# Attention and a leaky-ReLU MLP on one core: more blocks by seven products, keys transposed in place, and a written order for five stages

## The chip, the cores and the metric

The kernel runs on one core of one Trainium2 chip. The metric is the device time of one execution in microseconds (us); a run's time is compared with runs of the other kernel on the same chip. Five engines matter here: TensorE (PE in the profile, its weight loads PEld), VectorE (DVE), ScalarE (ACT), GpSimd (POOL, which issues the loads from DRAM) and SyncE (SP, which issues the DMA transposes and the stores). All transfers share 16 DMA engines.

## The reference

```python
def _attn_ref(q, k, v, is_retrieval, n_sink, window):      # q, k, v: 4 x 8 x 768 x 64
    scores = scale * np.matmul(q, k.transpose(0, 1, 3, 2))
    ...
    causal = rel >= 0
    stream_keep = causal & (is_sink | in_win)              # 4 sinks, window of 64
    mask = np.where(retr[0, :, 0, 0, None, None], full_mask, stream_mask)
    scores = np.where(mask[None, :, :, :], scores, -1000000000.0)
    ...
    return np.matmul(a, v)                                 # a: softmax of the scores

def _moe_ref(x, w_in, w_out):                              # 3072 x 512, 512 x 2048, 2048 x 512
    h = x @ w_in
    g = np.maximum(0.01 * h, h)
    return (g @ w_out)
```

Heads 0, 2 and 6 see all earlier positions; the five others see four sinks and a window of 64. The attention's output, heads side by side, is x of the MLP.

## The kernel before, in words

**Tiling.** The 3072 rows are cut into eight chunks of 384 queries, numbered 0 to 7 in the order of the list `ORDER`: chunks 0 and 2 are the two halves of batch 0, 1 and 3 of batch 1, 4 and 5 of batch 2, 6 and 7 of batch 3. Everything is bf16 with fp32 accumulation in eight PSUM banks, two under each of four tags (`ph`, `psS`, `po`, `py`).

**Stages.** From stage n = 2 on (the loop at the end of the kernel), stage n holds on TensorE, interleaved: the attention of chunk n + 1 (class `Attention`; its slots are "a" below), the first matmul of the MLP of chunk n (`in_slots`), and the second matmul of earlier chunks (`Pair`, whose half units are the list `outs`). The instructions of an engine run in the order in which the Python code writes them (the schedule is manual), and each DMA queue issues in that order too. The lists are mixed by `merge`, which spreads by estimated costs, and the last microseconds of a stage are set apart (`last_of`, `tail`, `keep`), with most attention slots ahead of them.

**The first matmul** comes in two forms. A tick (line 597) is 4 matmuls of 384 columns for 128 of the 2048 hidden units, emptied by one activation (line 600). A block of 512 hidden units can instead be made by seven products (class `Quad`, line 686): 7 units of 4 matmuls of 192 columns, with sums of weights (`in_sum`) and of activations (`x_sum`, four subtractions in `x_sums`, line 652), three ScalarE copies (700), three VectorE additions (714) and four activations (693). `BY_SEVEN` says which blocks are made so: two each of chunks 4, 6 and 7. A tick or a quad reads all of `xts[n]`, the transposed output of the attention of chunk n, four pieces of 384 columns, one for each pair of heads.

**How a chunk's x gets there.** When a pair of heads is through, `finish` takes a reciprocal and a product on VectorE (lines 423, 425), and `x_t` issues a DMA transpose from SP's queue (line 430). This is so from chunk 3 on (`cross=True`); earlier chunks are transposed on TensorE.

**Keys and queries.** `load_qk` (line 116) loads a chunk's keys and queries with GpSimd's queue, three DMAs each, into the single buffers `kb` and `qb`. `turn_dma` (line 248) transposes them from SP's queue into `kd` and `qd`. A matmul contracts over 128 partitions, two heads, so the keys of a head stand in a tile whose other 64 partitions are zero: `kt[i][0]` and `kt[i][1]` for even and odd heads of batches of parity i. `spreads` (line 264) copies the transposed keys from `kd` there by six VectorE copies per chunk, and for a new batch two small copies fill the sink keys `ksink` (lines 290 and 294). In stage n the order on SP's queue is: `turn_dma(n + 2)`, keys ahead of queries, then the x transposes of the attention of chunk n + 1, with the output stores (line 834) among them.

**GpSimd's queue** waits in order too: `load_qk(n + 3)` waits until the transposes of the chunk before have read the buffers, `load_v` (line 123) can be held back by a one-element copy (`hold`, lines 121 and 1173).

## Time and profile before

| | |
|---|---|
| time, median of 3 runs | 222.63 us (222.37 to 224.13) |
| profiled execution: span from first to last instruction | 219.4 us; the median run is 3.2 us longer (the profiled execution's own time outside the span is not given) |
| busy: PE / PEld / DVE / ACT / POOL | 212.3 / 168.7 / 144.5 / 147.0 / 72.6 us |
| DMA packets | 112732, 28.90 MB |
| stages 2, 3, 4 on TensorE | from 69.0, 89.6 and 109.3 us |
| stages 5, 6, 7 on TensorE, and the tail of `outs` | from 138.9, 159.3, 188.7 and 203.7 us |

How to read it: "L597 PE" is line 597 on TensorE. A matmul's own duration in the profile overlaps the next one's, so the pace of TensorE is read from the starts of successive rows (the chain of waits prints those), not from the mean duration. "DMA kd<-kb" is a transfer by the names of its tiles. The digits of a line in 40 slices are tenths of busy time in slices of 5.5 us.

### The profile page before, as it was taken

To read this page: it belongs to the slowest core of one execution; us is meant where nothing else is said; L and a number is where in the kernel's file an instruction comes from. 1 tells how busy PE (TensorE), PEld (TensorE's weight loads), DVE (VectorE), ACT (ScalarE), POOL (GpSimd) and SP (SyncE) were. 2 spreads that over 40 slices of the span, in tenths; PEclk is the share of its full clock that TensorE was granted. 3 is DMA by queue.
4 is the path that set the end of the run, shared out by engine and by line. 5 is a ranking of instruction groups with operands and counts; after the bars stand their busy time and mean duration, and the time that the engine had idled before them with its cause. 6 is when DMAs were issued, how large, how long until landed. Compare 5 with 4: busy or idle time off the path is not lost.

```text
span 219.4 us, 6062 instructions
## 1 busy us (share of the span) xinstructions
PE 212.3 (97%) x2432; PEld 168.7 (77%) x2432; DVE 144.5 (66%) x392; ACT 147.0 (67%) x335; POOL 72.6 (33%) x91
## 2 busy tenths in 40 slices
PE   7799999999999999999999999999999999999993
PEld 5579775688888777876688888777787888878893
DVE  6685886949699696757267875664473846626653
ACT  4766956743876996477679786687478886567220
POOL 8998542059406906309056402700000000000000
PEclk9999999999999999999999999999999999999999
DMA  9999999999999999999999996993320131200222
GB/s 131 150 174 180 178 207 190 174 170 143 174 98 255 178 141 150 155 227 125 152 170 158 136 143 176 156 183 51 81 96 16 55 87 21 96 0 3 96 107 89
DMA packets 112732, 28.90 MB, mean 132 GB/s; under 512 B 102208, under 2 KB 109760, under 8 KB 112704
## 3 DMA queue, kind: packets, MB, share of 16 engines
q0 software_dynamic: 78080, 13.37, 85.0%
q1 hardware_dynamic: 33280, 14.65, 35.4%
q10 hardware_dynamic: 1344, 0.50, 1.2%
q8 instruction: 19, 0.31, 0.6%
q14 instruction: 9, 0.07, 0.1%
HBM read 27.30 MB, written 6.29 MB: 153 GB/s over the span
## 4 chain that ended last, share of the span: by engine, by line
PE 88%; DMA 6%; POOL 2%; DVE 1%; issue 1%; POOLq 0%
PE ph L597 26%; PE py L800 20%; PE po L326 8%; PE py L779 8%; DMA va<-in_v_dram 6%; PE psS L357 5%; PE ph L686 4%; PE psS L392 3%; PE psS L597 2%; PE po L779 2%; PE po L800 2%; PE ph L779 1%; POOL va L123 1%; PE psS L686 1%; PE po L686 1%; PE psS L779 1%
## 5 line engine op out<-in xcount | busy, mean ns | idle before, releaser
L597 PE MATMUL ph<-xt,w_in_bf 128*128 128x384 bf16 x352 | 68.9, 326 | 0.0
L600 ACT ACTIVATE g_all<-ph 128x384 bf16<-128x384 f32 x88 | 43.4, 493 | 21.1 <-PE ph L597 18.5
L597 PEld LDWEIGHTS <-w_in_bf 128*128 128x128 bf16 x384 | 34.0, 97 | 17.4 <-issue 0.9
L362 ACT ACTIVATE at<-psS 128x384 bf16<-128x384 f32 x76 | 36.0, 490 | 9.0 <-PE psS L357 5.7
L800 PEld LDWEIGHTS <-sum 128*128 128x128 bf16 x256 | 23.8, 98 | 4.1
L116 POOL DMA_DIRECT2D kb<-in_k_dram x21 | 18.6, 908 | 20.9 <-DMA kd<-kb 20.4
L357 PE MATMUL psS<-qd,kt 128*128 128x384 bf16 (+2 forms) x90 | 23.0, 294 | 0.0
L123 POOL DMA_DIRECT2D va<-in_v_dram x24 | 21.4, 914 | 0.9 <-DVE xs L573 0.7
L116 POOL DMA_DIRECT2D qb<-in_q_dram x21 | 18.7, 920 | 3.9 <-DMA w_in_bf<-in_moe_w_in_dram 1.7
L326 PE MATMUL po<-va,at 128*128 128x65 bf16 x228 | 19.6, 194 | 0.3 <-DMA va<-in_v_dram 0.3
L800 PEld LDWEIGHTS <-g_all 128*128 128x128 bf16 x192 | 18.0, 98 | 2.3
L401 DVE TENSOR_TENSOR ats<-ats,m_win 128x384 bf16<-128x384 bf16 x35 | 13.1, 375 | 10.0 <-ACT ats L397 9.8
L800 PE MATMUL py<-w_sum,sum 128*128 128x256 bf16 x120 | 17.7, 272 | 0.0
L326 PEld LDWEIGHTS <-at 128*128 128x128 bf16 x234 | 14.4, 98 | 3.8 <-issue 0.5
L397 ACT ACTIVATE ats<-psS 128x384 bf16<-128x384 f32 x33 | 16.0, 494 | 1.8 <-PE psS L392 1.5
L761 DVE TENSOR_TENSOR sum<-g_all 128x1024 bf16<-128x1024 bf16 x24 | 16.4, 684 | 0.0
L800 PE MATMUL py<-w_out_bf,g_all 128*128 128x256 bf16 x112 | 16.1, 272 | 0.0
L800 PE MATMUL py<-w_out_bf,sum 128*128 128x256 bf16 x120 | 15.7, 273 | 0.0
L425 DVE TENSOR_TENSOR xs<-po,linv 128x384 bf16<-128x384 f32 x27 | 15.1, 558 | 0.9
L779 PEld LDWEIGHTS <-sum 128*128 128x128 bf16 x152 | 13.1, 98 | 1.6 <-issue 0.2
L264 DVE COPY kt<-kd 64x512 bf16<-64x512 bf16 x36 | 12.7, 362 | 1.3 <-DMA kd<-kb 0.9
L326 PEld LDWEIGHTS <-ats 128*128 128x128 bf16 x210 | 10.3, 97 | 2.5 <-DVE ats L401 0.2
(244 smaller groups left out, 402.0 us busy)
## 6 DMA issues: line engine op xcount, KB each, us to landing
out_dram<-o SPq DMA_DIRECT2D x23, 256.0 KB, 3.7
va<-in_v_dram POOLq DMA_DIRECT2D x24, 128.0 KB, 6.9
kb<-in_k_dram POOLq DMA_DIRECT2D x21, 128.0 KB, 6.5
qb<-in_q_dram POOLq DMA_DIRECT2D x21, 128.0 KB, 6.7
w_out_bf<-in_moe_w_out_dram POOLq DMA_DIRECT2D x4, 512.0 KB, 12.4
vb<-va SPq DMA_DIRECT2D x8, 170.6 KB, 3.6
w_in_bf<-in_moe_w_in_dram POOLq DMA_DIRECT2D x2, 512.0 KB, 8.3
w_in_bf<-in_moe_w_in_dram POOLq DMA_DIRECT2D x4, 256.0 KB, 7.9
```

What stands on the lines that cost most here:

```text
L116: nc.gpsimd.dma_start(out=t[:, g], in_=nat[nm][b, c, :, :, g])
L123: nc.gpsimd.dma_start(out=va[b][:, 3 * c + g, :, 0:D], in_=nat["v"][b, c, :, :, g])
L326: nc.tensor.matmul(o, lhsT=lhsT, rhs=rhs, start=first, stop=False, skip_group_check=True)
L357: nc.tensor.matmul(s[:, off : off + w], lhsT=kt[i][hh][:, p, 128 * kj : 128 * kj + 128], rhs=q_of(n, p, lo, CH), start=(j == 0), stop=(j = ...
L362: nc.scalar.activation(out=a[:, 0:off], in_=s[:, 0:off], func=ACTF.Exp, scale=SM)
L397: nc.scalar.activation(out=av_, in_=s[:, 0:CH].rearrange("p (j e f) -> p j e f", j=3, e=2), func=ACTF.Exp, scale=SM)
L425: nc.vector.tensor_tensor(xs[:], po[:, :, :, 0:D], linv.to_broadcast([128, 3, 2, D]), op=ALU.mult)
L597: nc.tensor.matmul(ph[:, 0:CH], lhsT=w_in_bf[:, g, 128 * t : 128 * t + 128], rhs=xts[n][:, g, :] if n else xts[0][:, :, g, :], start=(g == ...
L600: nc.scalar.activation(out=g_all[:, slab(n) : slab(n) + 3, t, :], in_=ph[:, 0:CH].rearrange("p (j t) -> p j t", j=3), func=ACTF.Prelu, alp ...
L761: nc.vector.tensor_tensor(self.s[i], x, y, op=op)
L779: nc.tensor.matmul(s[:, 0 : c1 - c0], lhsT=lhs[:, j, :], rhs=rhs[:, j, c0:c1], start=first and j == 0, stop=(j == NH - 1), skip_group_chec ...
L800: nc.tensor.matmul(s, lhsT=lhs[:, j, :], rhs=rhs[:, j, :], start=u in ("P1", "P2", "P5") and j == 0, stop=(j == NH - 1), skip_group_check= ...
```

## The change

1. `BY_SEVEN` gets two blocks each of chunks 3 and 5: four quads replace sixteen ticks. Each of the two chunks needs its `x_sums`.
2. The keys of chunks 4 to 7 are loaded by six DMAs, even and odd heads apart, into one tile `kz` whose other halves are zeroed once (two memsets on VectorE after the copies of chunk 3's keys). Three DMA transposes, each of eight 128 x 128 blocks where there were four, write straight into `kts`. The VectorE copies of `spreads` are gone for these chunks; the two copies of sink keys stay. `kz` takes the memory of the two `kd` buffers. The keys of chunk 4 are loaded after the memsets, at the end of the part ahead of the loop, and not with its queries; the keys of chunks 5 to 7 wait for the transposes of the chunk before to have read `kz`.
3. Stages 3 to 7 are no longer mixed by `merge`: `WOVEN` writes out their order, one letter for an item: a an attention slot, p a half unit of `outs`, t a tick, A and B the units of the two quads, x the four subtractions of `x_sums`, e a copy of sink keys, v the shift of V (in stage 4, the transposes of chunk 7's keys).
4. In woven stages a quad runs its products in another order, puts P2, P5 and P3 into one bank under the tag `po`, and adds P5 straight from that bank.

```diff
--- before.py
+++ after.py
@@ -79,7 +79,10 @@
     m_win0 = bf("m_win0", 6, 64)
     m_sink = one.tile([128, H], FP32, name="m_sink")
     hold = bf("hold", 1)
-    kt = [[bf(f"kt{i}_{hh}", 4, S) for hh in range(2)] for i in range(2)]
+    kts = [bf(f"kt{i}", 4, 2, S) for i in range(2)]
+    kt = [[t[:, :, hh, :] for hh in range(2)] for t in kts]
+    kz = bf("kz", 3, 4, 2, 128)
+    halves = [kz.rearrange("p g q h t -> p (g q h t)")[:, 1536 * i : 1536 * i + 1536] for i in range(2)]
     va = [bf(f"va{i}", 6, H, D + 1) for i in range(2)] * 2
     vb = [bf(f"vb{i}", 5, H - 1, D + 1) for i in range(2)] * 2
     vs = [bf(f"vs{i}", H, D + 1) for i in range(2)]
@@ -95,7 +98,7 @@
 
     raw = {}
 
-    k0 = rot.tile([128, 3, H, D], BF16, name="k0", tag="kd", bufs=2)
+    k0 = halves[0].rearrange("p (g h d) -> p g h d", g=3, h=H)
     q0 = rot.tile([128, 3, H, D], BF16, name="q0", tag="qd", bufs=3)
     f0 = {nm: rot.tile([128, DM], FP32, name="o", tag="o", bufs=4).rearrange("p (h d) -> p h d", h=H) for nm in ("k", "q")}
 
@@ -110,6 +113,12 @@
     def load_qk(n, nms="kq"):
         b, c = ORDER[n]
         for nm in nms:
+            if nm == "k" and n > 3:
+                for g in range(3):
+                    w = kz[:, g].rearrange("p q h t -> p (q h t)").rearrange("p (q x) -> p q x", q=4)
+                    for hh in range(2):
+                        nc.gpsimd.dma_start(out=w[:, :, 192 * hh : 192 * hh + D], in_=nat[nm][b, c, :, hh:H:2, g])
+                continue
             t = rot.tile([128, 3, H, D], BF16, name=f"{nm}b", tag=f"{nm}b", bufs=1)
             raw[nm, n] = t
             for g in range(3):
@@ -237,8 +246,16 @@
             move(eng, kt[0][h][:, :, 128 * j : 128 * j + 128], pt[:], h)
 
     def turn_dma(n, nms="kq"):
+        b, c = ORDER[n]
         for nm in nms:
-            dst = rot.tile([128, 3, 4, 128], BF16, name=f"{nm}d", tag=f"{nm}d", bufs=3 if nm == "q" else 2)
+            if nm == "k" and n > 3:
+                for g in range(3):
+                    o = CH * c + 128 * g
+                    nc.sync.dma_start_transpose(out=kts[b % 2].rearrange("p q h t -> p (q h) t")[:, :, o : o + 128],
+                                                in_=kz[:, g].rearrange("p q h t -> p (q h t)"))
+                continue
+            dst = rot.tile([128, 3, 4, 128], BF16, name="qd", tag="qd", bufs=3) if nm == "q" else \
+                halves[n % 2].rearrange("p (g q t) -> p g q t", g=3, q=4)
             if nm == "q":
                 qx[n] = dst
             else:
@@ -263,7 +280,7 @@
             o = CH * c + 128 * g
             nc.vector.tensor_copy(kt[b % 2][hh][r, :, o : o + 128], raw["kx", n][r, g])
 
-        order = [(g, hh) for hh in range(2) for g in range(3)] if n == 3 else [(g, hh) for g in range(3) for hh in range(2)]
+        order = [] if n > 3 else [(g, hh) for hh in range(2) for g in range(3)] if n == 3 else [(g, hh) for g in range(3) for hh in range(2)]
         r = [lambda g=g, hh=hh: spread(g, hh) for g, hh in order]
         if c == 0:
             r += sink_keys_by(b)
@@ -484,8 +501,9 @@
                 self.at = rot.tile([128, H, 128], BF16, name="at8", tag="sum", bufs=6)
             else:
                 self.blocks = [(kj, h) for kj in range(j, -1, -1) for h in RETR] + [None]
-                tag, bufs = ("sum", 6) if j == 1 else ("kd", 2)
-                self.at = rot.tile([128, len(self.blocks), 128], BF16, name="at_first", tag=tag, bufs=bufs)
+                n = len(self.blocks)
+                self.at = rot.tile([128, n, 128], BF16, name="at_first", tag="sum", bufs=6) if j == 1 else \
+                    halves[1][:, 0 : 128 * n].rearrange("p (n t) -> p n t", n=n)
 
         def key(self, h, k0):
             return kt[0][h % 2][:, h // 2, k0 : k0 + 128]
@@ -581,7 +599,14 @@
 
 
     done = [0] * NCH
-    BY_SEVEN = {4: (0, 1), 6: (0, 1), 7: (0, 1)}
+    BY_SEVEN = {3: (0, 1), 4: (0, 1), 5: (0, 1), 6: (0, 1), 7: (0, 1)}
+    WOVEN = {
+        3: "xaptpAAapaAtAaAapaAAAapBtaapptBaBtpBBataBBtBpppvaaapppt",
+        4: "pxaAapppAatpaAatAApaepAaApaatpaaAtpaaBBapaBtpaBapBppaeppaBpBpatapatppavptpppBpp",
+        5: "xaaAAptpaAatAAapaApAttaaBApBaBptBaapptpvaaBpptpaBBpBtp",
+        6: "xppaaAptAaappAaAtAapaApaatpaaBtAaapBApaaptppaaBppBBapatBpBaaptppBppaappppptp",
+        7: "txAtppAptpApBAttBApBpBAABtpBptpBtpBpApp",
+    }
 
     def slab(n):
         return 4 if n % 2 else n // 2 % 2
@@ -602,6 +627,8 @@
 
         ks = BY_SEVEN.get(n, ())
         ticks = [costing(0.65, lambda t=t: tick(t)) for t in range(NG) if t // 4 not in ks]
+        if n in WOVEN:
+            return {"t": ticks, **{"ABCD"[j]: Quad(n, k, ("psS" if j < 2 else "ph") if n + 1 == NCH else "ph", True).slots() for j, k in enumerate(ks)}}
         if n + 1 == NCH:
             several = [Quad(n, k, tag).slots() for k, tag in zip(ks, ("psS", "po", "ph"))]
             if len(ks) > 2:
@@ -651,24 +678,31 @@
         for i, y, z in ((1, b(0, 1), b(0, 0)), (2, b(1, 1), t[:, 0]), (3, b(1, 1), b(0, 1)), (4, b(1, 0), t[:, 1])):
             nc.vector.tensor_tensor(t[:, i - 1], y, z, op=ALU.subtract)
         x_sum[n] = t
-        if n + 1 == NCH:
-            temps[n] = [rot.tile([128, 2, CH], FP32, name=nm, tag=tag, bufs=bufs) for nm, tag, bufs in
-                        (("p1s", "kd", 2), ("us", "kd", 2), ("u3s", "kb", 1))]
+        if n in (6, 7) and len(BY_SEVEN[n]) > 0:
+            three = [t.bitcast(FP32).rearrange("p (x t) -> p x t", x=2) for t in
+                     (*halves, rot.tile([128, 1536], BF16, name="u3s", tag="kb", bufs=1)[:])]
+            temps[n] = [[t[:, x] for t in three] for x in range(2)]
+
 
     class Quad:
 
 
-        def __init__(self, n, k, tag):
-            self.n, self.k, self.tag = n, k, tag
+        ORDERS = (("P1", "P6", "P7", "P4", "P2", "P5", "P3"), ("P1", "P2", "P6", "P5", "P7", "P4", "P3"))
+
+        def __init__(self, n, k, tag, woven=False):
+            self.n, self.k, self.tag, self.woven = n, k, tag, woven
             self.bank, self.late = {}, []
 
         def slots(self):
-            return [costing(0.33, lambda u=u: self.unit(u)) for u in ("P1", "P6", "P7", "P4", "P2", "P5", "P3")] + [costing(0.0, lambda: self.late.pop()())]
+            return [costing(0.33, lambda u=u: self.unit(u)) for u in self.ORDERS[self.woven]] + [costing(0.0, lambda: self.settle())]
+
+        def settle(self):
+            while self.late:
+                self.late.pop()()
 
         def unit(self, u):
             n, k = self.n, self.k
-            while self.late:
-                self.late.pop()()
+            self.settle()
             t = x_sum[n]
             x = xts[n].rearrange("p g (j e t) -> p g j e t", j=3, e=2)
             b = lambda a, e: x[:, KH * a : KH * a + KH, :, e, :]
@@ -678,8 +712,10 @@
                             "P7": (q(3), t[:, 2], "y"), "P5": (q(1), t[:, 0], "x"), "P4": (w(1, 1), t[:, 3], "y"),
                             "P3": (q(4), b(1, 1), "x")}[u]
             first = u in ("P1", "P2", "P5")
-            if first:
-                self.bank[at] = bank(self.tag, [128, 512], FP32)
+            if u == "P5" and self.woven:
+                self.bank[at] = self.bank["a"]
+            elif first:
+                self.bank[at] = bank("po" if u == "P2" and self.woven else self.tag, [128, 512], FP32)
             s = self.bank[at]
             for m in range(2):
                 for g in range(KH):
@@ -696,23 +732,25 @@
             if not self.left:
                 done[self.n] += 4
 
+        def add(self, u, s):
+            t, m, e = {"P2": (self.p1, 0, 0), "P5": (self.u3, 1, 1), "P3": (self.u, 0, 1)}[u]
+            nc.vector.tensor_tensor(t, s, t, op=ALU.add)
+            self.late.append(lambda: self.out(t, m, e))
+
         def empty(self, u, s):
-            copy = lambda o: nc.scalar.activation(out=o, in_=s, func=ACTF.Copy)
             if u == "P1":
                 self.left = 4
-                self.p1, self.u, self.u3 = (t[:, self.k] for t in temps[n]) if n in temps and self.k < 2 else \
-                    (rot.tile([128, CH], FP32, name=nm, tag=nm, bufs=1)[:] for nm in ("p1q", "uq", "u3q"))
-                copy(self.p1)
-            elif u == "P6":
-                copy(self.u)
-            elif u == "P7":
-                copy(self.u3)
-            elif u == "P4":
+                own = temps.get(self.n, ())
+                self.p1, self.u, self.u3 = own[self.k % 3] if self.k % 3 < len(own) else \
+                    [rot.tile([128, CH], FP32, name=nm, tag=nm, bufs=1)[:] for nm in ("p1q", "uq", "u3q")]
+            if u in ("P1", "P6", "P7"):
+                nc.scalar.activation(out={"P1": self.p1, "P6": self.u, "P7": self.u3}[u], in_=s, func=ACTF.Copy)
+            if u == "P4":
                 self.out(s, 1, 0)
-            else:
-                t, m, e = {"P2": (self.p1, 0, 0), "P5": (self.u3, 1, 1), "P3": (self.u, 0, 1)}[u]
-                nc.vector.tensor_tensor(t, s, t, op=ALU.add)
-                self.late.append(lambda: self.out(t, m, e))
+            elif u == "P7" and self.woven:
+                self.add("P5", self.bank["x"][:, 0:CH])
+            elif u in ("P2", "P3") or u == "P5" and not self.woven:
+                self.add(u, s)
 
     def in_tile(t0, j, tag="ph", nt=4):
         ph = bank(tag, [128, 4, 128], FP32)
@@ -1093,7 +1131,7 @@
     run(p1[:14], steps(0, ("P1",)), p1[14:])
     fourth = weight_sums(1)
     turn_dma(3)
-    load_qk(4)
+    load_qk(4, "q")
     run(steps(1, ("P1",)))
     run(steps(0, ("P2", "P6")))
     fourth()
@@ -1115,6 +1153,9 @@
     turn_thirds(3, (1, 2), "psS", "a")
     sp, keep = spreads(3), tail(m2[at:], a2[-7:])
     run(keep[:-5], sp[:3], keep[-5:], sp[3:])
+    for hh in range(2):
+        nc.vector.memset(kz[:, :, :, hh, 64 - 64 * hh : 128 - 64 * hh], 0.0)
+    load_qk(4, "k")
     load_v(4)
 
     for n in range(2, NCH):
@@ -1125,7 +1166,7 @@
                 sink_values(ORDER[n + 2][0], nc.gpsimd)
             turn_dma(n + 2, "q" if n == 5 else "kq")
             if n == 3:
-                load_v(n + 2, behind=raw["kx", n + 2][0:1, 0, 0, 0:1])
+                load_v(n + 2, behind=kt[ORDER[n + 2][0] % 2][0][0:1, 0, CH * ORDER[n + 2][1] : CH * ORDER[n + 2][1] + 1])
             if n == 4:
                 v_shift(n + 2)
             extra = spreads(n + 2)
@@ -1133,10 +1174,27 @@
                 load_qk(n + 3, "k" if n > 2 else "kq")
         if n + 1 < NCH:
             a = Attention(n + 1, cross=True).slots(lag=2 if n > 3 else 3)
-            a = into(a, extra) if n > 2 else a
+            a = into(a, extra) if n > 2 and n not in WOVEN else a
         if n == 2:
             a = [(lambda f=f, i=(6, 9, 12, 15).index(j): (f(), in_sums(0, i + 1))) if j in (6, 9, 12, 15) else f for j, f in enumerate(a)]
         ins = in_slots(n)
+        if n in WOVEN:
+            lists = {"a": a, "p": outs, "x": [lambda: x_sums(n)], "e": [], "v": [lambda: v_shift(n + 2)], **ins}
+            if n > 2:
+                lists["e"] += extra
+            if n == 4:
+                lists["v"] = [lambda: turn_dma(7, "k")]
+            if n == 5 and len(BY_SEVEN.get(7, ())) > 2:
+                lists["e"] += [lambda i=i: in_sums(1, i + 1) for i in range(4)]
+            for c in WOVEN[n]:
+                lists[c].pop(0)()
+            assert not any(lists[c] for c in "aptABCDe" if c in lists)
+            if n in (3, 4):
+                nc.gpsimd.tensor_copy(hold[0:1, :], xts[n + 1][0:1, 3, 0:1])
+                load_qk(n + 3, "q")
+                load_v(n + 3)
+            outs = [f for k in range(3 * n // 2, 3 * n // 2 + 1 + n % 2) for f in steps(k)]
+            continue
         if n == 7:
             x_sums(n)
         if n == 3:
@@ -1156,7 +1214,7 @@
             at = last_of(ms, 3.5)
             ms, keep = ms[:at], tail(ms[at:-2], a[-3:]) + ms[-2:]
             keep.insert(2, lambda: v_shift(4, nc.scalar))
-            a = a[:-7] + [f for i in range(4) for f in (a[i - 7], *extra[2 * i : 2 * i + 2])]
+            a = a[:-7] + [f for i in range(4) for f in (a[i - 7], *extra[i : i + 1])]
         elif a:
             at = last_of(ms, 3.2 if n == 3 else 5.8)
             ms, keep = ms[:at], ms[at:]
```

## The prediction

> **What bounds the kernel now.** I read the page first, then TensorE's waits, then the chain of waits, then busy time by stage.
>
> ```profile
> span 219.4 us, 6062 instructions
> PE 212.3 (97%) x2432; PEld 168.7 (77%) x2432; DVE 144.5 (66%) x392; ACT 147.0 (67%) x335; POOL 72.6 (33%) x91
> DMA  9999999999999999999999996993320131200222
> ```
>
> ```profile
> PE psS L156 <- DVE first L939: 1.1, 1, 1.1
> ```
>
> This is TensorE's longest wait, in the opening; the same view from 30 us on has no row at all. A busy TensorE could still be a slow one, so the pace must be seen in the chain:
>
> ```profile
> 132.29 0.65 PE ph L597 x4
> 132.94 0.33 PE ph L686 x4
> 133.27 0.44 PE py L800 x4
> ```
>
> Each row starts where the one before ends. TensorE streams without gaps here. So a gain can come only from columns that are not streamed, and any wait put on TensorE adds in full. The stages concerned:
>
> ```profile
> core 0: us, PE busy (x) PEld busy (x) DVE busy (x) ACT busy (x) POOL busy (x), PEclk, DMA share, GB/s
> 89.60:109.30 19.70, 19.70 (x214) 14.35 (x213) 11.11 (x32) 14.14 (x31) 5.51 (x7) 1.00 1.64 167
> 109.30:138.90 29.60, 29.60 (x351) 24.85 (x349) 20.71 (x53) 21.57 (x51) 12.14 (x16) 1.00 1.56 153
> 138.90:159.30 20.40, 20.40 (x220) 15.12 (x219) 10.81 (x33) 14.10 (x32) 2.41 (x3) 1.00 0.96 117
> ```
>
> These are stages 3, 4 and 5: TensorE is full in all three, at full clock, and stage 4, which has two quads already, is as full as stage 3, which has none. A better written order has nothing to win there. The other number to keep is the DMA share, over 1 until stage 5: transfers queue behind one another.
>
> **The change part by part.** *Four quads for sixteen ticks.* A tick is 0.65 us (first row of the chain above), four of them 2.60. A unit of a quad is 0.33, seven 2.31. Each quad saves 0.29, four save **1.2 us**. What empties their banks:
>
> ```profile
> L600 ACT ACTIVATE g_all<-ph 128x384 bf16<-128x384 f32 x88 | 43.4, 493 | 21.1 <-PE ph L597 18.5 <-PE po L326 1.1 <-DVE at L367 0.3
> L700 ACT ACTIVATE uq<-ph 128x384 f32<-128x384 f32 x4 | 2.0, 495 | 0.4 <-PE ph L686 0.4
> L714 DVE TENSOR_TENSOR uq<-ph,uq 128x384 f32<-128x384 f32 x4 | 2.2, 552 | 1.2 <-PE ph L686 1.2
> L652 DVE TENSOR_TENSOR x_sum<-xt 128x384 bf16<-128x384 bf16 x6 | 2.1, 350 | 0.0
> L264 DVE COPY kt<-kd 64x512 bf16<-64x512 bf16 x36 | 12.7, 362 | 1.3 <-DMA kd<-kb 0.9
> ```
>
> On ScalarE a quad costs three copies and four activations of nearly the same shape, 7 x 0.5 = 3.5 us, for four activations of 0.49: 1.5 more, 3.1 more in stages 3 and 5. ScalarE goes from 14.1 of 19.7 us (72%) to about 17.2 of 19.1 (90%). VectorE gets 6 x 0.55 and 4 x 0.35 per chunk, 4.7 us, and loses 6 x 0.36, 2.2: 2.5 more, about 71%. I cost both at nothing, because TensorE is the cover and both stay below it; P5 starts in the bank of P2 and so waits for the addition (0.55); the written order puts P6 and another item, 0.66 us or more, between them. If bursts break that cover, the nearest row is one activation late, 0.5 us, a few times: 0 to 1.5 us, of which I take 0.
>
> *The copies of keys go.* VectorE was not the bound, so the 24 copies (8.7 us) are worth nothing by themselves.
>
> *The keys of chunk 4 start later.* The memsets stand behind the last copies of chunk 3's keys, and the load stands behind the memsets.
>
> ```profile
> 70.10 1.52 DVE L264 COPY kt<-kd 64x512 bf16<-64x512 bf16 x3
> ```
>
> ```profile
> 68.00 2.63 POOL L116 DMA_DIRECT2D kb<-in_k_dram  x3 [10.61 <-DMA kd<-kb]
> 70.59 2.66 POOL L116 DMA_DIRECT2D qb<-in_q_dram  x3
> 73.19 2.70 POOL L123 DMA_DIRECT2D va<-in_v_dram  x3
> 84.22 2.70 POOL L116 DMA_DIRECT2D kb<-in_k_dram  x3 [7.38 <-DMA kd<-kb]
> ```
>
> ```profile
> L183 DVE MEMSET kt<- 64x768 uint32 x4 | 2.8, 698 | 0.8 <-issue 0.8
> L140 POOL DMA_DIRECT2D w_in_bf<-in_moe_w_in_dram x6 | 4.6, 776 | 0.3 <-issue 0.2
> ```
>
> The copies end at 71.6. A memset of kt is 768 words in 0.70 us, one of kz 384 words, so two take 0.8: 72.4. Queries now go first, at 68.0. Six half-sized key DMAs follow; each issue lies between 0.45 (half of 0.9) and 0.9, and w_in's 0.78 is the nearest: 72.4 to 77.0. The values of chunk 4 come behind, 4 us later than before. A key load was in flight 5.9 us:
>
> ```profile
> kb<-in_k_dram POOLq DMA_DIRECT2D x3, 128.0 KB, 5.9
> ```
>
> Two DMAs make a third. The second of the first third is issued at 73.2 and lands at 79.1, that of the last at 76.2 and 82.1.
>
> ```profile
> 73.79 3.96 SPq L248 DMA_TRANSPOSE kd<-kb  x3
> 78.28 4.11 SPq L248 DMA_TRANSPOSE qd<-qb  x1
> 82.50 6.84 SPq L430 DMA_TRANSPOSE xt<-xs  x4
> ```
>
> SP's queue, which issued the first row at 73.8, now waits until 79.1. Behind the waiting transposes stand the queries' transposes and all four x transposes of chunk 3. The issue took about 1.3 us each, the queries' one 4.1 while the queue was full. So the keys end at 83.4, the queries at 84.7 to 87.5, and three x transposes at 88.6 to 91.4. The fourth was ready at 88.0 before (the product below plus its 0.56): SP holds it up by 0.6 to 3.4 us, or by nothing if the loads land a little sooner. I take 0, since SP has no other work then.
>
> How long eight blocks fly no row shows. Alone, three blocks took 2.3 us and twelve 3.7 (rows below); I take 3.2 alone, and the crowded 7.3 as the upper end. For chunks 5 to 7 the longer issue on GpSimd (4.6 us for 2.7) and on SP hides in idle time: the table of stages has GpSimd busy for 12.1 of 29.6 us in stage 4 and 2.4 of 20.4 in stage 5.
>
> *A tick stands fourth in stage 3.* Before, ten half units of `outs` stood ahead of the first tick of chunk 3; now the order is x, a, p, t.
>
> ```profile
> 85.23 0.25 PE L326 MATMUL po<-va,at 128*128 128x65 bf16 x3
> 86.90 0.26 PE L326 MATMUL po<-vs,at_sink 128*128 128x65 bf16 x3
> 89.61 0.33 PE L357 MATMUL psS<-qd,kt 128*128 128x384 bf16 x1
> 96.01 0.81 PE L597 MATMUL ph<-xt,w_in_bf 128*128 128x384 bf16 x4
> ```
>
> ```profile
> 87.42 0.56 DVE L425 TENSOR_TENSOR xs<-po,linv 128x384 bf16<-128x384 f32 x1
> ```
>
> Attention of chunk 3 ends at 87.0, its last product at 88.0, and its transpose was issued at once. Stage 3 starts at 89.61; a score (0.16) and a half unit (0.44) later, at **90.2**, TensorE stands at the tick, which needs that transpose. It had time until 96.0 before. How long does it fly? Two answers, for 88.0 to 88.1 and for 133 to 134:
>
> ```profile
> q0 software_dynamic: 117, 0.01, 76.0%
> xt<-xs SPq DMA_TRANSPOSE x1, 6.6
> ```
>
> ```profile
> xt<-xs SPq DMA_TRANSPOSE x1, 2.3
> ```
>
> and, for the four of chunk 3 together:
>
> ```profile
> DMA to landing us min/median/max: 3.8/5.2/6.6
> ```
>
> Beside loads it took 6.6 us, alone 2.3. With 6.6 it lands at 94.6, and TensorE waits **4.4 us**; with 2.3, at 90.3, 0.1; with 6.6 and SP 3.4 late, at 98.0, 7.8. I take 6.6, the row of this very transfer: loads of chunk 5 are again in flight, and twelve more key blocks stand ahead of it. VectorE waits with it, since x is first in its queue, but the masks behind x belong to slots that TensorE reaches later.
>
> The Trainium skill ("DMA: Bandwidth & Descriptors", queues, rings and completion order) says that each DMA engine takes turns, packet by packet, between the queues that have work. By that alone a transpose beside one loading queue should need about twice its lone time, 4.6 us, an estimate; the wait would be 2.4 and the total 223.8 us. The 6.6 of this trace is longer, since its own queue was not empty either.
>
> *Later boundaries.* At 3 to 4, three half units and a tick (2.0) and then about 2.6 us stand between the last slot and the first unit that needs the last transpose; product and flight take 1.0 + 2.3 to 6.6: 0 to 3.0. I take 0, because the code holds GpSimd's next loads until this very transpose has landed, so it should fly nearly alone. Into 5 to 7 the distance is 3.3 to 4.8 against the lone 3.3: 0.
>
> **Sum** on the profiled execution: 219.4 - 1.2 + 4.4 = 222.6 us of span, 3.2 up. The median run stands 3.2 us above the span, so **225.8 us**.
>
> **The rivals.** *A. The last x transpose flies almost alone.* Keys of chunk 5 may be loaded only after the transposes of chunk 4's keys have read `kz`, so GpSimd could start them later than 84.2, and its own load queue could be nearly empty at 88. For it: the lone 2.3 at 133, and the 3.8 of an earlier one of these four. Against it: first transposes that land by 84 release those loads just then. It decides when the flight is under 3.4 us (a wait under 1.2); then the wait is 0.1 to 1.2, and the time 221.5 to 222.6: not slower, slightly faster. I put 222.0.
>
> *B. The sink-key copy blocks VectorE.* The two copies now wait for the transposes themselves, in VectorE's order ahead of the last masks of stage 2.
>
> ```profile
> 81.47 0.58 DVE L264 COPY kt<-kd 64x512 bf16<-64x512 bf16 x2
> 82.31 0.23 DVE L367 TENSOR_TENSOR at<-at,m_caus 128x128 bf16<-128x128 bf16 x1 [0.27 <-ACT at L362]
> ```
>
> ```profile
> kd<-kb SPq DMA_TRANSPOSE x3, 7.3
> kd<-kb SPq DMA_TRANSPOSE x1, 3.7
> ```
>
> VectorE would stand at the copy at 81.5. The first third, issued at 79.1, lands at 82.3 by the lone 3.2 or at 86.4 by the crowded 7.3. The values that need the mask were multiplied at 85.2 (row above), and copy and mask take 0.6, so it decides from a landing at 84.6 on. At the crowded end TensorE loses 1.8 us, and one mask more behind the second copy, 2.5 in all, ahead of stage 3; the x transpose is as much later, with the same wait behind it: 225.8 + 2.5 = 228.3 us.
>
> *C. ScalarE becomes the bound* in stages 3 and 5, 90% busy with two banks for each use: 1.5 us on top of a short wait at the tick, 224 to 227.
>
> **How the numbers follow.** A measurement of this kernel tells about 1% from no change, 2.2 us: 220.4 to 224.9. Forecast 0.45, with waits of 2.5 to 6 us, of which 0.10 fall below 224.9; A 0.32, all within 1%, save 0.02 beyond it; B 0.15, slower; C 0.08, half of it slower. Faster 0.02, within 1% 0.44, slower 0.54. Range: from A's lower end, 221.3, to a little above B, 229.0. The forecast's own range is 223.9 to 227.4.
>
> **What would show it.** Right: a TensorE gap of 3 to 6 us at the first line 597 of stage 3, ended by the DMA xt; stage 4 to 7 without gaps; quad units at 0.33 us; SP waiting for the key load until about 79. Wrong: no gap there (A), a VectorE wait at line 290 for the key transposes with a TensorE gap before stage 3 (B), gaps spread over stages 3 and 5 that end with ScalarE (C), or a span shorter than 218 us, which no term of mine allows.

## The result, and the profile after

The kernel after took **230.73 us** (median of 6 runs, 228.94 to 232.5) beside 223.38 us (222.11 to 228.0) for the kernel before in the same comparison: ratio 1.033, with a 95% interval of 1.0269 to 1.0392. It is slower by 7.35 us. (Times here and below are medians over all runs of a kernel, while the ratios leave out runs of more than 1.5% above its fastest, so the two can differ by a few tenths of a per cent.) The forecast was 225.8, with a range that ended at 229.0. The sign was right, the size was too small.

The profiled execution took 231.75 us, of which 229.5 are span, 10.1 more than before. From its page: the span, the busy times, and the line of the clock in 40 slices.

```profile
span 229.5 us, 6197 instructions
PE 216.1 (94%) x2480; PEld 173.8 (76%) x2480; DVE 146.4 (64%) x390; ACT 149.4 (65%) x347; POOL 80.3 (35%) x103
...
PEclk9999999999999999859999999999999999999999
```

The line of the clock has a notch: slices 17 and 18 show 8 and 5 where all others show 9. TensorE was busy longer than before, though it streams fewer columns. This is the first sign that something other than a wait was added. TensorE's waits from 30 us on, a view that had no row at all before:

```profile
PE ph L622 <- DMA xt<-xs: 6.5, 5, 2.1
```

Line 622 is the tick (597 before). Where those waits lie, TensorE's timeline shows (start, length, instruction, idle time before it in brackets):

```profile
90.76 0.60 PE L838 MATMUL py<-w_out_bf,g_all 128*128 128x256 bf16 x4
93.45 0.34 PE L622 MATMUL ph<-xt,w_in_bf 128*128 128x384 bf16 x1 [2.09 <-DMA xt<-xs]
95.10 0.32 PE L622 MATMUL ph<-xt,w_in_bf 128*128 128x384 bf16 x1 [1.32 <-DMA xt<-xs]
96.17 0.48 PE L622 MATMUL ph<-xt,w_in_bf 128*128 128x384 bf16 x1 [0.74 <-DMA xt<-xs]
97.51 0.48 PE L622 MATMUL ph<-xt,w_in_bf 128*128 128x384 bf16 x1 [0.86 <-DMA xt<-xs]
97.78 1.06 PE L838 MATMUL py<-w_out_bf,g_all 128*128 128x256 bf16 x4
98.64 0.84 PE L722 MATMUL ph<-xt,w_in_bf 128*128 128x192 bf16 x4
99.28 0.84 PE L722 MATMUL po<-xt,w_in_bf 128*128 128x192 bf16 x4
...
171.41 0.32 PE L622 MATMUL ph<-xt,w_in_bf 128*128 128x384 bf16 x1 [1.51 <-DMA xt<-xs]
```

The first tick of stage 3 stands fourth, as written, and each of its four matmuls waits for its own piece of x. The half unit of `outs` ahead of it is done at 91.2 (90.76 and 0.44); the next unit starts at 97.78, where 91.85 was due. Then see what follows: the two units of a quad stand 0.64 us apart (98.64 to 99.28), not 0.33. TensorE is running at half speed. Busy time by stretch, with the granted clock in the column ahead of the last two:

```profile
95.70:102.50 6.80, 5.47 (x32) 4.00 (x32) 2.81 (x8) 2.71 (x7) 1.00 (x2) 0.50 1.54 238
102.90:116.00 13.10, 13.10 (x171) 11.00 (x169) 7.76 (x21) 11.42 (x29) 5.86 (x8) 1.00 1.26 108
116.00:146.00 30.00, 30.00 (x362) 24.86 (x360) 19.36 (x48) 21.99 (x53) 11.20 (x14) 1.00 1.62 151
146.00:169.20 23.20, 23.20 (x276) 19.58 (x274) 15.18 (x40) 17.27 (x43) 5.49 (x7) 1.00 1.34 163
```

For 6.8 us the clock was 0.50. After that the rest of stage 3 and stages 4 and 5 are as full as before: the quads themselves cost TensorE no waits here, although ScalarE is busy for 11.42 of 13.10 us (87%).

I took the start of every matmul against the pace of its form (0.162 us for 384 columns, 0.109 for 256, 0.082 for 192, and so on), so that columns, gaps and slow clock come apart:

| span of the profiled execution | us |
|---|---|
| before | 219.4 |
| columns streamed: 112 matmuls of 192 columns for 64 of 384 | -1.2 |
| gaps at the first tick of stage 3, 0.2 to 5.8 | +5.6 |
| matmuls at half clock | +2.4 |
| gap at the tick of stage 6 | +1.7 |
| first 30 us | +0.7 |
| rest, each piece under 0.4, and rounding | +0.9 |
| after | 229.5 |

These are the sizes of one execution. In a second profile of the kernel after (part 9) the gaps at the tick of stage 3 came to 3.5 us and the half clock to 1.6, and other waits stood in their place.

### The profile page after: what moved, and what is told of

It reads as the page before. It is cut to its first block, busy times and chain, and to the rows that moved or that the text cites. A ratio compares the mean times of both kernels' runs of the same rounds, so it can differ in the third digit from the quotient of the medians.

```text
span 229.5 us, 6197 instructions
## 1 busy us (share of the span) xinstructions
PE 216.1 (94%) x2480; PEld 173.8 (76%) x2480; DVE 146.4 (64%) x390; ACT 149.4 (65%) x347; POOL 80.3 (35%) x103
## 4 chain that ended last, share of the span: by engine, by line
PE 82%; DMA 11%; DVE 3%; POOL 2%; issue 1%; ACT 0%; POOLq 0%
PE ph L622 19%; PE py L838 19%; PE po L343 7%; PE py L817 7%; DMA va<-in_v_dram 6%; PE psS L374 5%; DMA xt<-xs 5%; PE ph L722 5%; PE po L722 4%; PE psS L622 2%; PE psS L409 2%; PE po L817 2%; PE po L838 2%; PE ph L817 1%; PE psS L722 1%; POOL va L132 1%
## 5 line engine op out<-in xcount | busy, mean ns | idle before, releaser
L622 PE MATMUL ph<-xt,w_in_bf 128*128 128x384 bf16 x288 | 59.1, 328 | 6.5 <-DMA xt<-xs 6.5
L625 ACT ACTIVATE g_all<-ph 128x384 bf16<-128x384 f32 x72 | 35.5, 493 | 28.9 <-PE ph L622 27.2
L622 PEld LDWEIGHTS <-w_in_bf 128*128 128x128 bf16 x320 | 29.1, 98 | 18.7 <-issue 3.4
L379 ACT ACTIVATE at<-psS 128x384 bf16<-128x384 f32 x76 | 35.4, 492 | 11.7 <-PE psS L374 8.7
L120 POOL DMA_DIRECT2D kz<-in_k_dram x24 | 18.1, 782 | 11.0 <-DMA kt<-kz 10.7
L838 PEld LDWEIGHTS <-g_all 128*128 128x128 bf16 x192 | 18.5, 100 | 4.2 <-issue 1.4
L838 PE MATMUL py<-w_out_bf,g_all 128*128 128x256 bf16 x112 | 16.9, 283 | 0.0
L838 PE MATMUL py<-w_sum,sum 128*128 128x256 bf16 x120 | 16.9, 273 | 0.0
L838 PE MATMUL py<-w_out_bf,sum 128*128 128x256 bf16 x120 | 16.4, 273 | 0.0
L722 PEld LDWEIGHTS <-in_sum 128*128 128x128 bf16 x160 | 13.6, 99 | 1.1
L722 PEld LDWEIGHTS <-w_in_bf 128*128 128x128 bf16 x120 | 10.6, 101 | 2.9 <-issue 1.7
```

Source lines behind the costliest of these rows:

```text
L120: nc.gpsimd.dma_start(out=w[:, :, 192 * hh : 192 * hh + D], in_=nat[nm][b, c, :, hh:H:2, g])
L379: nc.scalar.activation(out=a[:, 0:off], in_=s[:, 0:off], func=ACTF.Exp, scale=SM)
L622: nc.tensor.matmul(ph[:, 0:CH], lhsT=w_in_bf[:, g, 128 * t : 128 * t + 128], rhs=xts[n][:, g, :] if n else xts[0][:, :, g, :], start=(g == ...
L625: nc.scalar.activation(out=g_all[:, slab(n) : slab(n) + 3, t, :], in_=ph[:, 0:CH].rearrange("p (j t) -> p j t", j=3), func=ACTF.Prelu, alp ...
L722: nc.tensor.matmul(s[:, 192 * m : 192 * m + 192], lhsT=lhs[:, g, 128 * m : 128 * m + 128], rhs=rhs[:, g], start=first and m == 0 and g == ...
L838: nc.tensor.matmul(s, lhsT=lhs[:, j, :], rhs=rhs[:, j, :], start=u in ("P1", "P2", "P5") and j == 0, stop=(j == NH - 1), skip_group_check= ...
```

## The experiments

The theory: the tick's place costs the time, twice. TensorE waits there for the last x transpose, whose flight is long because loads share the DMA engines, and the broken idle time then halves the clock. The rivals: the new way of loading the keys makes SP late, and with the old way the wait goes; the flight is long because of SP's own queue; the quads cost ScalarE and VectorE too much in any order; and the half clock has nothing to do with the wait. Ratios are against the kernel before on the same chip. The edits are shown against the kernel after, unless said otherwise; "..." marks what is left out.

**1. The same idle time, filled.** Fifty matmuls whose results nobody reads go ahead of the tick (the kernel does more than the reference asks).

```diff
-        3: "xaptpAA...
+        3: "xapitpAA...
+            def fill():
+                s = bank("ph", [128, 512], FP32)
+                for _ in range(50):
+                    nc.tensor.matmul(s[:, 0:256], lhsT=ident[:], rhs=w_in_bf[:, 0, 0:256], start=True, stop=True)
...
```

> The changed kernel with 50 matmuls of 256 columns, whose result nobody reads, put on TensorE just ahead of the first tick of stage 3, 5.5 us of work where it sat idle. Theory T (the half clock of the next 5 to 7 us comes from the idle time): the x transpose lands as before, the record shows no half clock, and the time falls by 2.3 us, to 228 to 229 us. Rival (the clock falls for another reason): the half clock stays and the time is 230 to 232 us.

Measured: 229.39 us, ratio 1.0273 (1.0205 to 1.0341), span 227.4; the time is 0.4 above the range that was expected. TensorE's timeline and its clock:

```profile
92.37 5.62 PE L1185 MATMUL ph<-w_in_bf,ident 128*128 128x256 bf16 x50
97.83 0.81 PE L622 MATMUL ph<-xt,w_in_bf 128*128 128x384 bf16 x4
...
98.91 0.49 PE L722 MATMUL ph<-xt,w_in_bf 128*128 128x192 bf16 x4
99.24 0.49 PE L722 MATMUL po<-xt,w_in_bf 128*128 128x192 bf16 x4
```

```profile
98.00:104.00 6.00, 6.00 (x74) 5.04 (x73) 2.61 (x7) 5.03 (x13) 3.25 (x5) 1.00 1.46 177
```

The last x transpose lands at 96.8, while the fill still runs; the units behind the tick stand 0.33 us apart, and the clock is 1.00. From the tick's last matmul to the one that ends the half clock in the kernel after, the same instructions take 5.1 us there (97.51 to 102.62) and 2.7 here (98.31 to 101.00). So the half clock comes from the idleness, and it costs 2.4 us, as the table says. The difference of the spans, 2.1 us, is not that number: this profile has no wait in stage 6, but one of 1.4 us for x in stage 7, and others ahead of stage 3.

**2. The keys as before, the order as written.** Keys of chunks 4 to 7 are loaded in three DMAs and spread by VectorE; the key copies ("e") stand in the written orders.

```diff
-            if nm == "k" and n > 3:
+            if False:
...
-    load_qk(4, "q")
+    load_qk(4)
```

> The changed kernel with the keys of chunks 4 to 7 as before: loaded early into one buffer, transposed into two others, spread by VectorE copies, whose places in the written order are the only change of it. Theory T: SP's queue is free at 88 us, the last x transpose of chunk 3 is issued 2.6 us sooner, and as it flies 6 us or so beside the loads, TensorE still waits 3.5 to 4.5 us at the tick, perhaps with less of the half clock: 226 to 228 us. Rival K (the key chain alone is the cause): no wait at the tick and about 222 us. Rival O (the place of the tick alone is the cause, whatever SP does): 230 us as now.

Measured: 228.35 us, ratio 1.0217 (1.0145 to 1.0288), span 227.0. TensorE's waits from 30 us on, and the x transposes of chunk 3 on SP (lengths of the issues, first and last start, flights):

```profile
PE ph L622 <- DMA xt<-xs: 4.3, 2, 3.3
```

```profile
L447 SPq DMA_TRANSPOSE xt<-xs x4: 1197/1474/2126, 85.3 to 90.1; - x4
...
DMA to landing us min/median/max: 5.0/6.2/7.4
```

The same view of the kernel after:

```profile
L447 SPq DMA_TRANSPOSE xt<-xs x4: 1205/1460/1862, 86.5 to 91.6; - x4
...
DMA to landing us min/median/max: 5.9/6.3/6.6
```

That both land at 97.5 is chance, since this execution runs 1.1 us later: the last product of chunk 3 ends at 90.0 here and at 89.0 in the kernel after, and TensorE reaches the tick at 92.3 and at 91.2. Counted from that product, the last x transpose is issued after 0.1 us instead of 2.6, flies 7.4 us instead of 5.9, and lands after 7.5 us instead of 8.5. The gaps at the tick are 4.8 us for 5.8, and the half clock stays (6.8 us from 94.9 on). So in this pair of profiles SP's lateness is worth about 1 us of the wait; the rival that the late keys are the cause of it falls. The time is 0.35 us above the theory's range. (The wait in stage 6 is absent here; so it is in parts 1 and 4, which have the new keys.)

**3. Loads held back.** GpSimd's loads of chunk 5's keys and queries wait until chunk 3's last x transpose has landed.

```diff
-                load_qk(n + 3, "k" if n > 2 else "kq")
+            if 2 < n < NCH - 3:
+                load_qk(n + 3, "k")
...
+        if n == 2:
+            nc.gpsimd.tensor_copy(hold[0:1, :], xts[n + 1][0:1, 3, 0:1])
+            load_qk(n + 3)
```

> The changed kernel with GpSimd's loads of chunk 5's keys and queries held until the last x transpose of chunk 3 has landed. Theory T2: the transposes of chunk 3's x share the DMA engines with these loads; without them the last one flies 2.5 to 4.5 us, not 5.9, TensorE's wait at the tick falls from 5.8 to 2 to 4.5 us and the half clock shrinks or goes: 226 to 228 us here. It may return part of that at the start of stage 4, where chunk 5's keys come later. Rival Q (the transpose waits for its own queue, not for loads): the flight stays near 6 us and the time near 229 us.

Measured: 231.56 us, ratio 1.0308 (1.0209 to 1.0408), span 229.9. The same view of the x transposes, and TensorE's waits:

```profile
L447 SPq DMA_TRANSPOSE xt<-xs x4: 1206/1390/1612, 86.2 to 90.9; - x4
...
DMA to landing us min/median/max: 2.6/2.9/3.6
```

```profile
PE psS L374 <- DMA qd<-qb: 2.8, 1, 2.8
PE po L343 <- DMA vb<-va: 2.1, 1, 2.1
PE ph L622 <- DMA xt<-xs: 1.5, 1, 1.5
PE ph L722 <- DMA xt<-xs: 1.4, 1, 1.4
```

SP issued the same transposes in the same order at nearly the same times, and they flew 2.6 to 3.6 us instead of 5.9 to 6.6. So the loads make this flight long, not SP's own queue. The wait at the tick of stage 3 is gone (line 622's one wait is in stage 6). But chunk 5's queries now come late for stage 4, which starts with 2.8 and 1.4 us of idle time and 6.8 us of half clock. The wait moved; the flight came out as expected, the time (226 to 228 us) did not.

**4. The tick later.** Ten half units of `outs` and seven slots of attention stand ahead of the first product and the first tick, nearly as in the kernel before.

```diff
-        3: "xaptpAAapaAtAaAapaAAAapBtaapptBaBtpBBataBBtBpppvaaapppt",
+        3: "appappappapapapapxAAtaAtAaAtAAAatBBtaBptBatBpBBBvaaapppt",
```

> The changed kernel with another order of stage 3 alone: seven attention slots and nine half units stand ahead of x and of the first product or tick, where one of each stood. Theory T (TensorE waits at the first tick of stage 3 for the last x transpose, 5.8 us, and then runs about 5 us at half clock, 2.3 us): the wait falls under 1 us, the clock stays full, and the time falls by 7 to 8 us, to about 223 us. Rival K (the keys of chunk 4 arrive late and hold up all that follows, wherever the tick stands): the wait moves to other instructions of stage 3 and the time stays above 227 us. Rival S (stage 3 with its quads is short of ScalarE): waits for ScalarE take the place, over 226 us.

Measured: 228.27 us, ratio 1.0226 (1.0134 to 1.0318), span 228.1. TensorE's waits from 97 to 122 us:

```profile
PE po L722 <- DMA xt<-xs: 1.8, 1, 1.8
PE po L343 <- DMA vb<-va: 0.4, 1, 0.4
PE ph L722 <- DVE x_sum L679: 0.4, 1, 0.4
...
```

No wait at the tick, and full clock there. Instead, with the filling work used up early, the quads stand close together, and there are six short gaps, 2.2 us by the starts of matmuls: five for a bank that is not emptied in time, one for a subtraction of x. The quads are the same as in the kernel after, which has no such gap behind its tick, so how closely they stand matters. Stage 4 starts with a wait of 1.9 us for its own x. Most of the rest of the span went to a wait for shifted values at 59.9 us and half clock behind it, told of below. The time is that of rival S, not the 223 us of the theory, though ScalarE is only part of it.

**5. One part alone.** The kernel before with the new keys only, the lists mixed by cost as before:

```diff
-    BY_SEVEN = {3: (0, 1), 4: (0, 1), 5: (0, 1), 6: (0, 1), 7: (0, 1)}
+    BY_SEVEN = {4: (0, 1), 6: (0, 1), 7: (0, 1)}
...
-        if n in WOVEN:
+        if False:
```

> The kernel before with the padded keys of chunks 4 to 7 alone: no quads in chunks 3 and 5, no written order. Theory T2 (the loss has two parts: what stands at the edges of the stages while x transposes fly, and quads that crowd ScalarE and VectorE in stages 3 and 5; the keys themselves only make SP 2.6 us late once): ten half units cover the flight, VectorE has 8.7 us less, so 222.5 to 224.5 us, no difference. Rival K (the late, doubled key transposes cost by themselves): 225 us or more, with TensorE waiting for DMA in stages 3 and 4.

Measured: 225.0 us, ratio 1.0073 (1.0026 to 1.012), span 222.2, so a little slower, between the theory and rival K. TensorE does not wait for a DMA in stages 3 and 4. Its one longer wait from 30 us on, and VectorE just ahead of it:

```profile
PE po L343 <- DVE ats L418: 1.2, 1, 1.2
```

```profile
117.01 0.36 DVE L679 TENSOR_TENSOR x_sum<-xt,x_sum 128x384 bf16<-128x384 bf16 x1 [0.97 <-DMA xt<-xs]
```

At the start of stage 4 VectorE stands at a subtraction until an x transpose of chunk 4 has landed, and TensorE waits for the mask behind it. Two transposes of that chunk flew 8.6 and 8.8 us here, and 4.9 to 7.7 in the two profiles of the kernel before. So the new keys have a price of their own at this boundary, small beside the 3.3%; that the doubled key transposes make these flights longer is likely, and not tested.

And the kernel before with the four quads only (the edit is against the kernel before):

```diff
-    BY_SEVEN = {4: (0, 1), 6: (0, 1), 7: (0, 1)}
+    BY_SEVEN = {3: (0, 1), 4: (0, 1), 5: (0, 1), 6: (0, 1), 7: (0, 1)}
...
-            ms = outs[:10] + ins + outs[10:]
+            ms = outs[:10] + [costing(0.0, lambda: x_sums(3))] + ins + outs[10:]
...
+        elif n == 5:
+            ms = outs[:4] + [costing(0.0, lambda: x_sums(5))] + merge(ins, outs[4:-4]) + outs[-4:]
```

> The kernel before with the four quads of chunks 3 and 5 alone, mixed by cost as the other stages are; keys as before. Theory T2: the stream is 1.2 us shorter, but TensorE waits for the emptying of the quads' banks in stages 3 and 5, 3 to 5 us in many short pieces that end with ScalarE and VectorE, so 225 to 227.5 us. The prediction's term (quads save 1.2 us, ScalarE covered): 222 us.

Measured: 228.9 us, ratio 1.0246 (1.0188 to 1.0304), span 226.3. TensorE's waits from 97 to 115 us, and its busy time in stage 3:

```profile
PE ph L597 <- DVE uq L714: 0.9, 1, 0.9
PE ph L597 <- ACT g_all L600: 0.6, 3, 0.2
PE ph L686 <- ACT g_all L693: 0.4, 1, 0.4
```

```profile
89.60:112.50 22.90, 20.73 (x239) 16.41 (x237) 15.38 (x44) 15.04 (x34) 9.83 (x12) 1.00 1.75 162
```

Here nothing of keys or written order is in play, x is in time, and the four quads still make it 2.5% slower. They stream 1.2 us less and have gaps of 4.1 us in stage 3 and 1.9 in stage 5 (the kernel before: 0.2 in each), most in pieces of 0.3 to 1.1 us that end with a bank being emptied. Over the stretch ScalarE is busy for only 66%. So the cover fails in bursts, not on the mean. This is the forecast's third rival, at nearly four times the price that I gave it (5.6 us beyond the gaps of before, for 1.5), and worse than the 225 to 227.5 us expected here. One thing is left open: these quads also run their products in the old order and put them all into banks of `ph`, which the ticks use too (point 4 of the change).

**6. Quads and keys, mixed by cost.** As after, but without the written orders.

```diff
-        if n in WOVEN:
+        if False:
...
-            ms = outs[:10] + ins + outs[10:]
+            ms = outs[:10] + [costing(0.0, lambda: x_sums(3))] + ins + outs[10:]
```

> The changed kernel with stages 3 to 7 mixed by cost as before, not in the written order; the quads of chunks 3 and 5 and the padded keys stay (x_sums of chunk 3 behind ten half units, of chunk 5 behind four). Theory T: the ten half units ahead of the first product of chunk 3 cover the flight, 1.2 us are saved by the quads, a few tenths are lost at the edges: 221.5 to 223.5 us. Rival K: the late keys cost by themselves, over 225 us. Rival S: ScalarE at 90% in stages 3 and 5 costs 1 to 3 us, 223.5 to 226 us.

Measured: 228.87 us, ratio 1.0233 (1.0159 to 1.0306), span 227.7. I had expected 221.5 to 223.5, since the wait for x should go. It did go, and short waits for ScalarE and VectorE took its place: 3.3 us in stage 3, 1.8 in stage 4, 2.1 in stage 5. This miss led to the two runs of part 5. The edit undoes point 4 of the change together with the written order, so the run does not tell the two apart.

**7. All but stage 3's part.** Stage 3 as before; quads in 5, the keys and the written orders of 4 to 7 stay.

```diff
-    BY_SEVEN = {3: (0, 1), 4: (0, 1), 5: (0, 1), 6: (0, 1), 7: (0, 1)}
+    BY_SEVEN = {4: (0, 1), 5: (0, 1), 6: (0, 1), 7: (0, 1)}
-        3: "xaptpAAapaAtAaAapaAAAapBtaapptBaBtpBBataBBtBpppvaaapppt",
```

> The changed kernel with stage 3 as before (ticks only, mixed by cost, ten half units first) and all else as changed: quads in chunk 5, padded keys, written order in stages 4 to 7. Theory T2: the written order of stages 4 to 7 holds its quads without waits (the profile of the changed kernel has 0.4 us of gaps in stage 4 and 0.2 in most of 5), so the whole loss of stage 3 goes and 0.6 us of stream are saved: 222 to 223.5 us, no difference from before or slightly faster. Rival K: late keys still cost, 225 us and more.

Measured: 225.09 us, ratio 1.0049 (1.0002 to 1.0095). Leaving stage 3 alone takes back most of the loss, from 3.3% to 0.5%. The two quads that stay in stage 5 don't show as a gain: the 222 to 223.5 us expected were missed.

**8. Ways to a faster version.** First, stage 3 and the keys as before, quads and written order from stage 4 on, with three half units of stage 4 moved ahead of the unit that waited for x:

```diff
-        4: "pxaAapppAatpaAatAApaepAaApaatpaaAtpaaBBapaBtpaBapBppaeppaBpBpatapatppavptpppBpp",
+        4: "pxaAappppppAataAatAAaAaApaatpaaAtpaaBBeapaeBtpaeBapeBppaepepaBeepBpatapatppavptpppBpp",
...
```

> Stage 3 and the keys as before; quads in chunk 5 and the written order of stages 4 to 7 as changed, with three half units of stage 4 moved ahead of its unit P2, where the kernel without the change of stage 3 waited 1.5 us for an x transpose. Theory T2: none of the four losses is left (no late keys, no tick ahead of its transpose, no crowd in stage 3, no wait at P2), and two quads save 0.6 us of stream: 0.3% faster than before or no difference, ratio 0.994 to 1.003. Rival W (the written order of stages 4 to 7 costs by itself): ratio over 1.005.

Measured: 225.23 us, ratio 1.0103 (1.0057 to 1.0149). The wait for x at the start of stage 4 was gone, and the moved half units brought one of 1.2 us for a bank of the second matmul, emptied by VectorE, in its place. The ratio is rival W's. In the profile, though, 2.2 of the 3.4 us of added span are waits ahead of the written order (at 59.6 and 70.8 us), and stages 5 to 7 have no more gaps than before, so what the written order costs there is in stage 4. Second, the late tick with the old keys and this order of stage 4:

> The changed kernel with the keys as before, the ticks and products of stage 3 behind seven slots and nine half units, and stage 4's P2 behind three more half units: all waits for x transposes are covered, and the quads of stage 3 have to fit into its second half. Theory T2: ScalarE and VectorE are crowded there, and waits of 2 to 3 us for the emptying of banks are left: 224.5 to 226.5 us. Rival F (the flight of the x transposes is the only cause): 222 us, slightly faster than before.

Measured: 228.93 us, ratio 1.0269 (1.0218 to 1.032), so the old keys don't help the late tick; the 224.5 to 226.5 us expected were missed. No version beat the kernel before.

**9. Once more.** The kernel after, and the kernel before, on the same chip.

> The changed kernel once more, beside the others of this call. Theory T2: 229 to 232 us, waits for DMA xt at the first tick of stage 3 of 5 to 7 us in pieces, half clock behind them.

> The kernel before, profiled once more: does it have the wait at 59 us, for the shifted values of chunk 2 (2.1 to 2.6 us in five of the eight kernels run so far, none in the first profile), in a part of the program that the change does not reach? If it is a matter of the run, some profiles of the kernel before have it as well; the span is 219 to 223 us.

Measured: after 230.33 us, ratio 1.0335 (1.03 to 1.037), span 229.4; before 221.25, span 219.4. In this second profile of after the tick of stage 3 cost 3.5 us of gaps (last x issued at 91.5, landed at 96.7) and 3.4 us of half clock; the tick of stage 6 again 1.7; a wait of 2.0 us at 59.7 us and 1.7 us of waits at the start of stage 4 made up the difference. The time is as expected, the 5 to 7 us of waits at the tick are not.

**What stays open.** That wait at about 59.6 us is for the shifted values of chunk 2 (line 343, `vb`), in a part of the program that the change doesn't reach. It was 0.7 to 2.6 us in nine profiles (after_again and all variants but keys_alone and quads_alone), and absent in the first of after, both of before, and those two variants. The transfers are issued in the same order, the first at 52.0 to 53.8 us. I did not find what decides it, and tried nothing on it. The same holds for the wait in stage 6, which was there in both profiles of after and in the one with held loads, and in no other. Waits for x at other boundaries come and go as well (for instance in stage 4 of after_again, stage 5 of late_tick_old_keys and stage 7 of filled_wait, 1.2 to 1.9 us each), and so does a wait of 1.1 to 1.5 us for ScalarE at about 71 us, in filled_wait, quads_alone and stage3_and_keys_as_before. The interval of each comparison holds all this as noise, but a single span can carry 2 us of it, and 1.6 of half clock behind it, so the spans of two profiles can't be compared to better than that.

## Why the prediction was right in sign and wrong in size

The wait at the tick, on which the forecast rested, came. What failed is three terms that its sum held at nothing: the clock behind that wait, for which no step asked (2.4 us); SP's lateness at the last x transpose, taken as 0 (2.6 us, in part offset by a shorter flight); and the boundary into stage 6, taken as 0 (1.7 us). The span came out at 229.5 us for the 222.6 of the sum: 1.2 us more of gaps at the tick, 2.4 of half clock, 1.7 in stage 6, 0.7 in the first 30 us and 0.9 of small pieces. Term by term:

- *"TensorE streams without gaps", so only columns can be won and any wait adds in full.* Right. Four quads saved **1.2 us** of columns, as worked out.
- *The keys start later; SP waits until 79.1.* Right in the times: the memsets ended at 72.9 (72.4), the six loads were issued from 71.8 to 76.3, and SP's first key transpose was issued at 78.65. But the loads did not stand behind the memsets: the first was issued at 71.82, before the first memset began. From the timelines of VectorE, GpSimd and SP:

```profile
72.12 0.79 DVE L1157 MEMSET kz<- 128x384 uint32 x2
```

```profile
71.82 4.49 POOL L120 DMA_DIRECT2D kz<-in_k_dram  x6
```

```profile
78.65 6.21 SPq L254 DMA_TRANSPOSE kt<-kz  x3
```

- *"SP holds it up by 0.6 to 3.4 us … I take 0."* Wrong in value, though inside its range: the last x was ready at 89.0 (its product starts at 88.41 and takes 0.56) and issued at 91.6, 2.6 later. The flight was 5.9 for the assumed 6.6. All of stage 3 stood 1.0 us later than forecast; measured against it, the two make the landing 1.9 us later (2.6 less 0.7). The 4.4 us were counted to the last piece, but three of the tick's matmuls, 0.5 us, run ahead of it: the forecast's own landing meant 3.9 us of idle time, and by the starts of matmuls there were 5.8. In the run with the old keys the transpose was issued 2.5 us sooner after its product and landed 1.0 sooner, since it flew 1.5 longer: beside the loads, a lateness and a fixed flight don't simply add up.
- *The missing term.* No step of the forecast asked what idle time does to the clock. The half clock behind the wait cost **2.4 us** (1.6 in the second profile). The clock is in the page's slices, and the filled run shows that the wait causes it. The Trainium skill ("TensorE: Matmul & The Clock Gate", Part 1: The HAM clock gate) says that TensorE falls to half rate after an idle window of about 3.4 us and needs such a window of work to come back; by that rule a wait forecast at 4.4 us could have had 3.4 us of half clock behind it, up to 1.7 us more, an estimate. The traces agree on the lengths (3.4 and 6.8 us of half clock), but the window need not be idle from end to end, as the last section shows.
- *"Into 5 to 7 the distance is 3.3 to 4.8 against the lone 3.3: 0."* Wrong for stage 6, by **1.7 us**. Its last x transpose was issued behind two copies of shifted values and a store, 0.2 us after its product, and flew 5.0 us, not the lone 2.3. From SP's timeline, and from the DMA view of that moment:

```profile
166.38 1.23 SPq L447 DMA_TRANSPOSE xt<-xs  x1
```

```profile
xt<-xs SPq DMA_TRANSPOSE x1, 5.0
```

```profile
q1 hardware_dynamic: 962, 0.83, 59.4%
```

  The last line is the queue of SP's own transfers, from 166.4 to 171.4; GpSimd's loads (q0) have no packet in that time. So it didn't fly alone, and what it flew beside was what SP had issued just ahead of it. In filled_wait the same order gave 3.0 us; no run tested what decides it. Into stage 4 the 0 held in the first profile, and not in the second (waits for x of 1.2 us).
- *ScalarE at 90% costs 0.* Right for the written order only: 87% busy and no gap. The reason given was wrong. "TensorE is the cover and both stay below it" is an argument on the mean, and by it the mixed order would have been free too; there it cost 5.6 us. With the written order the gaps stay away. The late tick shows that the spacing of the units has a part in that (2.2 us of gaps with the same quads packed closer); how much is due to the other order of products and the other banks, no run separates.
- *Rival B, the sink-key copy.* VectorE did stand there, until 85.06, past the 84.6 from which the copy was to decide; TensorE had no gap, since its stage stood 1.0 us later than before. From VectorE's timeline:

```profile
85.06 0.18 DVE L307 COPY ksink<-kt 64x16 bf16<-64x16 bf16 x1 [1.23 <-DMA kt<-kz]
```

- *"The median run stands 3.2 us above the span."* It stood only 1.2 above it here, and the second profile of before ran in 221.25 at the same span of 219.4. The 3.2 held more than the time around the span, so the median hides 2 us of the miss in the span (6.9 us).
- *The range.* Its lower end, 221.3, is called that of rival A, which the text above it puts at 221.5.

What the change gives and takes, by the runs: the quads cost about 2.5% when mixed by cost, because the banks are not emptied in time. The written order, with the products and banks that go with it, holds them without gaps, but puts a tick fourth, which needs x before it can land; in the two orders tried with the tick further back, the quads stood closer and the gaps returned. In no form that was tried did the columns saved, 1.2 us or 0.6 with two quads, show as a gain.

## What to carry to other kernels

On an engine that streams without gaps, price a new wait with the clock that it costs behind it, and see whether other work could be put into the wait. Add up the idle time of a few microseconds, not only the longest gap. A flight depends on what is under way beside it (2.6 to 7.7 us for one and the same transpose here): take a range from several profiles, and not the one row. A mean of 66% or 87% busy on the engine that empties the banks says little: here the first had gaps and the second none.
